# GpSimd in source order, and masks formed from one broadcast of the decay logs per pair

## The chip, the cores and the metric

The kernel runs on one core of a Trainium2 chip. The metric is the device time of one execution in microseconds (us); of several runs the median is given. A core has a matrix engine (TensorE, PE in the views), a vector engine (VectorE, DVE), a scalar engine (ScalarE, ACT) and GpSimd (POOL). Each works through a queue of its own in a fixed order, and so does SyncE (SP), which only issues DMAs here. An instruction that waits holds up everything behind it in its queue. The PE clock has two levels, 1.2 and 2.4 GHz; the views give the granted clock as a share of 2.4 GHz, so that 0.50 is the lower level.

## The reference

Attention with a multiplicative decay for 8 batches x 8 heads, 576 tokens, head width 64, followed by a token-mixing and feed-forward block. What matters here, for one head:

```python
scores = (q @ k.T) / sqrt(D)
cum = cumsum(log(clip(f, 1e-4, 1.0)))          # running sum of the decay logs
scores = where(causal, -1e9, scores + cum[:, None] - cum[None, :])
attn = exp(scores - rowmax(scores)); attn /= attn.sum(-1)
x = attn @ v                                   # heads side by side: 576 x 512 a batch
h = x.T @ U @ V;  u = x + h.T
out = u + relu(u @ w_ch1) @ w_ch2
```

Within a row `cum[i]` is a constant that the softmax removes, so the kernel adds only the key's term `cum[j]` (scaled by -8) and the causal mask.

## The kernel before

Two heads make a **pair**, 32 pairs in all, four to a batch. `step(t)` handles pair p = t in ten slots s = 0 to 9: scores of row blocks 3, 1, 0 in slot 0 (`run_a`), of row block 2 and of the 64 tail rows in slot 3 (`run_b`), and the transposes of the exponentials P in slots 4 to 9 (`turn_p`). In the same ten slots it finishes the pair before, a = t - 1: the inverse of the row sums (`inverse`, tiles `sm` and `rv`) in slot 1, values in slot 3 (`values`), transposes back (`turn_x`, `turn_last`, tiles Tx and Tz) in slots 5 and 6, a split in high and low parts (`split_x`, tiles xh and xl) in slot 7 and the rank products (`ranks`, tile Tt) in slot 9. Matmuls of the feed-forward part of the batch before fill the slots (tiles A and B), and the first step after a batch's last pair also holds that batch's mixing (tiles H and Tu); steps 9, 13, 17, 21, 25 and 29 are such.

On VectorE, `top` (L290, L335) adds the mask tile to the scores in PSUM and finds the row extreme; ScalarE then forms P (L299). Each transposed block goes through a bank of the two-bank pool `psT` (tiles T) and is copied to `PT`, by ScalarE (first group) or VectorE (L366, the second and third groups). The division `rv` (L359) multiplies the result when Tx and Tz are taken out of their banks (L437, L402).

A pair's masks: four main tiles `M{p}_{i}` of 128 rows x 2 heads x 128(i+1) keys and one tail tile `M{p}_t`. `load_masks(p + 2)` in slot 5 has SyncE broadcast the logs from HBM (`cumd`) into each of them; each has two buffers, so a tile's DMA for pair p + 2 waits for `top` of pair p, which read that buffer. `triangles(p + 1)` in slots 4 and 7 has GpSimd write the masked triangle into the diagonal 128 columns (L142, L146).

`manual_schedule(engines=...)` names the engines whose queue keeps the order of the source. PE has it throughout, SyncE in step 0 and from step 8. VectorE, ScalarE and GpSimd are ordered by a list scheduler with estimates of its own, within the waits that the data need. So their queues aren't in the order in which the code is written.

Of the kernel before, what the change touches and what calls it, by code (L numbers as in the profile page):

```python
# [8 lines left out]
F32 = mybir.dt.float32  # L9
# [5 lines left out]
ALU = mybir.AluOpType  # L15
PSUM = bass.MemoryType.PSUM
ET = mybir.EngineType

B, H, S, D = 8, 8, 576, 64
# [3 lines left out]
P = 128  # L23
NHP = H // 2
NM = 4
MAIN = NM * P
TAIL = S - MAIN
# [7 lines left out]
MASKED = -8.0e9  # L35
# [6 lines left out]
def tile_decay_attention_moe(ctx, tc, qk, v, f, U, V, w1, w2, out):  # L42
    nc = tc.nc

    cumd = nc.dram_tensor("cumd", (B * H, S), F32, kind="Internal").ap()
# [45 lines left out]
    sb = pool("sb")  # L91
    sb2 = pool("sb2", 2)
# [8 lines left out]
    OWN = (slice(0, 64), slice(64, 128))  # L101
# [11 lines left out]
    make_identity(nc, ident)  # L113
    xn = [cst.tile([P, NM + 1, DM], F32, name=f"xn{i}") for i in range(NX)]

    def load_masks(p):
        if p >= NP:
            return
        z = st.setdefault(p, {"M": {}})
        for i in (3, 1, 0, 2):  # L120
            w = P * (i + 1)
            m = z["M"][i] = sb2.tile([P, 2, w], F32, tag=f"M{i}", name=f"M{p}_{i}")
            if p == 0:
                nc.gpsimd.memset(m, 0.0)
            else:
                src = cumd.rearrange("(j p) s -> p j s", j=2)[p, :, 0:w]
                nc.sync.dma_start(m, src.unsqueeze(0).broadcast_to([P, 2, w]))
        m = z["M"][NM] = sb2.tile([P, S], F32, tag="Mt", name=f"M{p}_t")
        if p == 0:
            nc.gpsimd.memset(m, 0.0)  # L130
            return
        for j in range(2):
            nc.sync.dma_start(m[OWN[j]], cumd[j * B * NHP + p].unsqueeze(0).broadcast_to([64, S]))

    def triangles(p, rows):
        if p >= NP:
            return
        for i in rows:
            m = st[p]["M"][i]
            if i < NM:  # L140
                d = m[:, :, P * i : P * i + P]
                nc.gpsimd.affine_select(d, d, [[0, 2], [-1, P]], ALU.is_ge, MASKED, base=0, channel_multiplier=1)  # L142
                continue
            for j in range(2):
                d = m[OWN[j], MAIN:S]
                nc.gpsimd.affine_select(d, d, [[-1, TAIL]], ALU.is_ge, MASKED, base=0, channel_multiplier=1)  # L146

    w1h = wt.tile([P, NA, NDC, P], F32R, name="w1h")
    w1l = wt.tile([P, NA, NDC, P], F32R, name="w1l")
# [72 lines left out]
    st = {}  # L222
# [405 lines left out]
    with tc.manual_schedule(engines=None):  # L628
        stay_awake(12)
        fr = sb.tile([P, S], F32, tag="xT", name="fr")  # L630
        fl = sb.tile([P, S], F32, tag="xh", name="fl")
        fl0 = sb2.tile([P, 10], F32, tag="sm", name="fl0")[:, 0:1]
        for j in range(2):
            nc.sync.dma_start(fr[OWN[j]], f)
        nc.scalar.activation(fl0, warm[:, 0:1], AF.Ln)
        load_qk(0)
        load_w(0)
        nc.vector.tensor_scalar(fr, fr, 1e-4, 1.0, op0=ALU.max, op1=ALU.min)
        nc.scalar.activation(fl, fr, AF.Ln)
        nc.scalar.activation(fl0, warm[:, 0:1], AF.Exp)  # L640
        picks = sb.tile([P, 2 * P], F32, tag="qkl", name="picks")
        n = B * NHP
        for rows, cols, col in (
            (OWN[0], slice(0, P), 0), (OWN[1], slice(0, P), 64 + n),
            (slice(0, P), slice(P, P + 64), 0), (slice(0, P), slice(P + 64, 2 * P), 64 + n),
        ):
            own = ident[rows, col : col + 1]
            nc.vector.tensor_scalar(picks[rows, cols], warm[rows, cols], own, -8.0, op0=ALU.mult, op1=ALU.mult)
        load_masks(0)
        triangles(0, range(NM + 1))  # L650
        nc.vector.tensor_tensor_scan(fr, fl, fl, 0.0, op0=ALU.add, op1=ALU.bypass)
        load_qk(1)
        load_w(1)
        nc.vector.tensor_scalar(fl[0 : B * H], fr[0 : B * H], -8.0, None, op0=ALU.mult)
        nc.sync.dma_start(cumd, fl[0 : B * H])
        load_masks(1)
        load_v(0)
        for i in range(NX - 1):
            nc.gpsimd.memset(xn[i][64:128, NM, :], 0.0)
# [29 lines left out]
    def step(t):  # L689
        p = SEQ[t]  # L690
        a = SEQ[t - 1] if t else None
        ps_, pa = p is not None, a is not None
        last, ending = t == LAST, t > LAST - 2
        nxt_p = p + 1 if ps_ else NP
        if ps_:
            z = st[p]
# [3 lines left out]
        for s in range(8 if last else SLOTS):  # L700
# [23 lines left out]
                stay_awake(1)  # L724
            if s == 4 and ps_ and p:
                load_v(p)
            if s == 4 and ps_:
                triangles(p + 1, (3, 1, 0))
            if s == 6 and ps_:
                load_qk(p + 2)  # L730
                if p == 0:
                    load_w(2)
                    load_w(3)
            if s == 5 and ps_:
                load_masks(p + 2)
            if s == 7 and ps_:
                triangles(p + 1, (2, NM))

            if ps_ and s == 0:
                run_a(p)  # L740
# [39 lines left out]
    pending = []  # L780
    ROOM = (1, 2, 3, 4, 5, 6, 8, 9)
    credit = [0.0]
    with tc.manual_schedule(engines={ET.PE, ET.SP}):
        step(0)
    with tc.manual_schedule(engines={ET.PE}):
        for t in range(1, 8):
            step(t)
    with tc.manual_schedule(engines={ET.PE, ET.SP}):
        for t in range(8, LAST + 1):
            step(t)  # L790
        run_later()
# [247 lines left out]
    z = {"g": order[0], "acc": xn[1], "po": [None] * NM, "done": [0] * NM}  # L1039
# [248 lines left out]
    with tc.manual_schedule(engines={ET.PE, ET.DVE, ET.Activation}):  # L1288
# [4 lines left out]
        s = 0  # L1293
# [8 lines left out]
        while batch_of(s) or queue or drains or any(x >= s for x in later):  # L1302
# [30 lines left out]
            for h, k, j, how in batch:  # L1333
                m = pairs[k].m
# [13 lines left out]
            for h, k, j, how in batch:  # L1348
                p = pairs[k]
# [7 lines left out]
            for h, k, j, how in batch:  # L1357
                p = pairs[k]
# [28 lines left out]
            while queue and queue[0][0] <= s and (credit > (1.0 if pairs[queue[0][1]].plain else 0.5)):  # L1387
                at, k, x = queue.pop(0)
                p = pairs[k]
# [63 lines left out]
```

## Time and profile before

| | |
|---|---|
| runs | 1456.59, 1459.94, 1461.51 us; median 1459.94 |
| profiled execution | 1459.31 us, of which its span is 1457.5 us |
| PE busy | 1221.3 us, 84% of the span |
| PEld (weight loads, overlap PE) | 1046.2 us, 72% |
| DVE busy | 841.4 us, 58% |
| ACT busy | 632.5 us, 43% |
| POOL busy | 257.8 us, 18% |
| mean granted PE clock | 0.915 |
| DMA | 218.76 MB, mean 150 GB/s |

Busy shares are averages over stages with different limits: the pairs run from 7 us to some 930 us, and the rest is the feed-forward part in another form. What each engine waits for has to be read stage by stage.

### The profile page before, as it was taken

The numbers are of one execution on the slowest core, as the hardware profiler recorded it, in microseconds if no ns is written. First come the engines' busy times: TensorE is split into PE (matmuls) and PEld (weight loads), VectorE is DVE, ScalarE is ACT, GpSimd is POOL, SyncE is SP. The second block draws the span as 40 slices with busy tenths as digits, with TensorE's granted clock in tenths as the row PEclk, the third lists the DMA queues.
The fourth block names the chain that finished last, engine by engine and source line by source line (L and its number), as shares of the span: only waits on it lengthen the run. The fifth ranks groups of instructions, "written<-read, shape, count | busy, mean of one in ns | idle before, by whom it ended". The sixth has DMA issues, their size and how long they took to land.

```text
span 1457.5 us, 24048 instructions
## 1 busy us (share of the span) xinstructions
PE 1221.3 (84%) x8465; PEld 1046.2 (72%) x8465; DVE 841.4 (58%) x2151; ACT 632.5 (43%) x1675; POOL 257.8 (18%) x423
## 2 busy tenths in 40 slices
PE   6554788777769768976876879999999999999998
PEld 3332567656567557765765657898788999999998
DVE  4464744533445434543443357698677678767775
ACT  3343444433334333442443335343455555555563
POOL 3343523112322222223212321000000000000000
PEclk8676798889979988988898989999999999999999
DMA  7855644655565565453352454459667575566534
GB/s 170 191 128 126 162 92 106 136 114 91 119 143 108 89 173 91 103 143 110 85 169 85 113 111 150 169 169 309 214 203 238 172 239 178 175 205 212 173 116 122
DMA packets 150281, 218.76 MB, mean 150 GB/s; under 512 B 17488, under 2 KB 83536, under 8 KB 148112
## 3 DMA queue, kind: packets, MB, share of 16 engines
q1 hardware_dynamic: 149888, 216.96, 55.3%
q8 instruction: 67, 1.10, 0.3%
q14 instruction: 54, 0.44, 0.1%
q10 hardware_dynamic: 272, 0.26, 0.1%
HBM read 169.84 MB, written 47.33 MB: 149 GB/s over the span
## 4 chain that ended last, share of the span: by engine, by line
PE 54%; DMA 25%; DVE 9%; issue 4%; ACT 4%; POOL 3%; SPq 1%; POOLq 0%; DVEq 0%; ACTq 0%
DMA M_t<-cumd 16%; PE pf L1093 13%; PE po L1185 7%; PE A L572 5%; PE B L590 5%; DMA M<-cumd 4%; PE V L420 4%; PE px L1185 3%; PE T L379 3%; ACT P L299 2%; PE pf L1185 2%; PE Tt L470 2%; PE Hb L916 2%; PE S_0c L278 1%; PE po L1200 1%
## 5 line engine op out<-in xcount | busy, mean ns | idle before, releaser
L379 PE MATMUL T<-ident,P 128*128 128x128 f32 x640 | 119.7, 318 | 159.7 <-DVE PT L366 150.9
L379 PEld LDWEIGHTS T<-ident,P 128*128 128x128 f32 x640 | 89.7, 164 | 182.6 <-issue 159.2
L1316 ACT COPY mc<-pf 128x512 f32<-128x512 f32 x139 | 81.5, 586 | 169.0 <-PE pf L1093 169.0
L142 POOL TENSOR_SCALAR_AFFINE_SELECT M<-M 128x256 f32<-128x256 f32 x128 | 52.6, 412 | 534.8 <-DMA M<-cumd 500.6
L572 PE MATMUL A<-uh,w1h 128*128 128x256 f32 (+1 forms) x384 | 124.2, 323 | 1.8 <-DVE hl L576 1.8
L420 PE MATMUL V<-PT,vr 128*64 128x448 f32 (+3 forms) x640 | 99.7, 453 | 22.4 <-ACT PT L364 18.9
L572 PE MATMUL A<-ul,w1h 128*128 128x256 f32 (+1 forms) x384 | 117.4, 306 | 0.3 <-DVE ul L510 0.3
L572 PE MATMUL A<-uh,w1l 128*128 128x256 f32 (+1 forms) x384 | 117.3, 306 | 0.0
L359 DVE RECIPROCAL rv<-sm 128x9 f32<-128x9 f32 x32 | 6.9, 215 | 176.2 <-POOL sm L358 176.2
L366 DVE COPY PT<-T 128x256 f32<-128x256 f32 (+1 forms) x192 | 73.6, 414 | 49.9 <-PE T L379 49.1
L590 PE MATMUL B<-w2h,hh 128*128 128x512 f32 x216 | 94.9, 439 | 3.3 <-DVE ost L604 3.3
L420 PEld LDWEIGHTS V<-PT,vr 128*64 128x64 f32 x640 | 42.6, 144 | 75.9 <-issue 37.5
L1244 POOL TENSOR_TENSOR xn<-xn,xn 128x512 f32<-128x512 f32 x1 | 1.3, 1267 | 529.8 <-DMA out_dram<-xn 529.8
L453 ACT CAST xh<-xn 128x640 fp32r<-128x640 f32 x32 | 23.2, 726 | 161.7 <-DVE xn L402 161.7
L590 PE MATMUL B<-w2l,hh 128*128 128x512 f32 x216 | 88.1, 408 | 0.0
L590 PE MATMUL B<-w2h,hl 128*128 128x512 f32 x216 | 87.8, 407 | 0.0
L572 PEld LDWEIGHTS A<-uh,w1h 128*128 128x128 f32 x384 | 76.7, 200 | 2.4 <-DVE hl L576 2.0
L576 DVE SCALAR_TENSOR_TENSOR hl<-A,hh 128x256 fp32r<-128x256 f32 (+1 forms) x96 | 43.4, 452 | 58.3 <-ACT hh L580 58.2
L572 PEld LDWEIGHTS A<-uh,w1l 128*128 128x128 f32 x384 | 76.9, 200 | 0.1
L572 PEld LDWEIGHTS A<-ul,w1h 128*128 128x128 f32 x384 | 76.4, 199 | 0.5 <-DVE ul L510 0.5
L160 POOL TENSOR_TENSOR qkl<-raw,qkh 128x1216 fp32r<-128x1216 f32 x26 | 72.1, 2772 | 20.5 <-ACT qkh L157 20.5
L1093 PE MATMUL pf<-d,b1h 128*128 128x256 f32 x320 | 69.6, 280 | 1.3 <-DVE fd L921 1.3
(322 smaller groups left out, 3904.2 us busy)
## 6 DMA issues: line engine op xcount, KB each, us to landing
un<-ud SPq DMA_DIRECT2D x16, 1024.0 KB, 7.0
M<-cumd SPq DMA_DIRECT2D x31, 512.0 KB, 5.8
d<-ud SPq DMA_DIRECT2D x48, 256.0 KB, 3.9
M<-cumd SPq DMA_DIRECT2D x31, 384.0 KB, 8.6
twd<-xn SPq DMA_DIRECT2D x40, 256.0 KB, 2.8
raw<-in_qk_dram SPq DMA_DIRECT2D x32, 288.0 KB, 7.8
Th<-twd SPq DMA_DIRECT2D x35, 256.0 KB, 3.6
tw<-twd SPq DMA_DIRECT2D x35, 256.0 KB, 2.8
```

Of the source, the lines that this page charges most:

```text
L142: nc.gpsimd.affine_select(d, d, [[0, 2], [-1, P]], ALU.is_ge, MASKED, base=0, channel_multiplier=1)
L160: leng.tensor_tensor(dl, src, dh.bitcast(F32), op=ALU.subtract)
L299: nc.scalar.activation(pt, ps, AF.Exp, bias=z["nm"][:, col : col + 1], scale=-1.0, accum_out=z["sm"][:, col : col + 1])
L366: defer(2, lambda: nc.vector.tensor_copy(dst, src))
L379: nc.tensor.transpose(tp[:, P * (x + c) : P * (x + c) + P], z["P"][j][i][:, P * c : P * c + P], ident)
L420: nc.tensor.matmul(ps, vr[:, c, j], pt[:, j, c, lo:hi], start=c == 0, stop=lo == 0)
L572: nc.tensor.matmul(ps[:, :nt], wt[:, fc, c], ut[:, c, sl], start=m == 0, stop=m == 3 * NDC - 1)
L576: nc.vector.scalar_tensor_tensor(hl[:, fc, :nt], ps[:, :nt], 0.0, hh.bitcast(F32)[:, fc, :nt], op0=ALU.max, op1=ALU.subtract)
L590: nc.tensor.matmul(ps, ht[:, fc, P * x : P * x + P], wt[:, fc], start=fc == 0 and m == 0, stop=fc == NA - 1 and m == 2,)
L1093: nc.tensor.matmul(ps, a[x][:, c], b[y][:, c], start=start and m == 0, stop=m == 5, skip_group_check=True)
L1185: nc.tensor.matmul(ps[:, HT * x : HT * x + HT], f[a][:, P * x : P * x + P], w[b], start=k.i == 0 and m == 0 and x == 0 and not (k.n == NG ...
L1316: nc.scalar.copy(mc, FA)
```

## The change

Two things. First, GpSimd is added to the engines that keep the source's order, in all steps. Second, SyncE broadcasts one tile a pair, `decay` (2 heads x 512 keys, two buffers), and GpSimd forms each of the four main masks from it with one `affine_select` that writes the whole tile, logs and triangle. The main mask tiles now have one buffer instead of two. The tail tile is broadcast as before. The masks of pair p + 1 are formed in slots 2, 3, 4, 6 and 8 of step p.

```diff
-    def load_masks(p):
+    def load_decay(p):
         if p >= NP:
             return
         z = st.setdefault(p, {"M": {}})
-        for i in (3, 1, 0, 2):
-            w = P * (i + 1)
-            m = z["M"][i] = sb2.tile([P, 2, w], F32, tag=f"M{i}", name=f"M{p}_{i}")
-            if p == 0:
-                nc.gpsimd.memset(m, 0.0)
-            else:
-                src = cumd.rearrange("(j p) s -> p j s", j=2)[p, :, 0:w]
-                nc.sync.dma_start(m, src.unsqueeze(0).broadcast_to([P, 2, w]))
+        z["decay"] = sb2.tile([P, 2, MAIN], F32, tag="decay", name=f"decay{p}")
         m = z["M"][NM] = sb2.tile([P, S], F32, tag="Mt", name=f"M{p}_t")
         if p == 0:
+            nc.gpsimd.memset(z["decay"], 0.0)
             nc.gpsimd.memset(m, 0.0)
             return
+        src = cumd.rearrange("(j p) s -> p j s", j=2)[p, :, 0:MAIN]
+        nc.sync.dma_start(z["decay"], src.unsqueeze(0).broadcast_to([P, 2, MAIN]))
         for j in range(2):
             nc.sync.dma_start(m[OWN[j]], cumd[j * B * NHP + p].unsqueeze(0).broadcast_to([64, S]))
 
-    def triangles(p, rows):
+    def mask(p, i):
         if p >= NP:
             return
-        for i in rows:
-            m = st[p]["M"][i]
-            if i < NM:
-                d = m[:, :, P * i : P * i + P]
-                nc.gpsimd.affine_select(d, d, [[0, 2], [-1, P]], ALU.is_ge, MASKED, base=0, channel_multiplier=1)
-                continue
-            for j in range(2):
-                d = m[OWN[j], MAIN:S]
-                nc.gpsimd.affine_select(d, d, [[-1, TAIL]], ALU.is_ge, MASKED, base=0, channel_multiplier=1)
+        z = st[p]
+        if i < NM:
+            w = P * (i + 1)
+            m = z["M"][i] = sb.tile([P, 2, w], F32, tag=f"M{i}", name=f"M{p}_{i}")
+            nc.gpsimd.affine_select(
+                m, z["decay"][:, :, 0:w], [[0, 2], [-1, w]], ALU.is_ge, MASKED, base=P * i, channel_multiplier=1
+            )
+            return
+        for j in range(2):
+            d = z["M"][NM][OWN[j], MAIN:S]
+            nc.gpsimd.affine_select(d, d, [[-1, TAIL]], ALU.is_ge, MASKED, base=0, channel_multiplier=1)
...
-            if s == 4 and ps_:
-                triangles(p + 1, (3, 1, 0))
+            if s in MASKS and ps_:
+                mask(p + 1, MASKS[s])
...
             if s == 5 and ps_:
-                load_masks(p + 2)
-            if s == 7 and ps_:
-                triangles(p + 1, (2, NM))
+                load_decay(p + 2)
...
-    with tc.manual_schedule(engines={ET.PE, ET.SP}):
+    MASKS = {2: 3, 3: 1, 4: 0, 6: 2, 8: NM}
+    with tc.manual_schedule(engines={ET.PE, ET.SP, ET.Pool}):
         step(0)
-    with tc.manual_schedule(engines={ET.PE}):
+    with tc.manual_schedule(engines={ET.PE, ET.Pool}):
         for t in range(1, 8):
             step(t)
-    with tc.manual_schedule(engines={ET.PE, ET.SP}):
+    with tc.manual_schedule(engines={ET.PE, ET.SP, ET.Pool}):
         for t in range(8, LAST + 1):
             step(t)
```

The queue of PE is the same row for row before and after. What moves on the others is shown at three places. The numbers that stand first in a name are the pair's (M9_3 is the mask of pair 9, row block 3; sm7 and rv7 the sums and inverse of pair 7); the last number is a buffer's.

GpSimd before, from the masks of pair 9 on:

```order
L142 AFFINE_SELECT M9_3_1875<-M9_3_1875 128x2x128
L142 AFFINE_SELECT M9_1_1877<-M9_1_1877 128x2x128
L142 AFFINE_SELECT M9_0_1879<-M9_0_1879 128x256
L160 TENSOR_TENSOR qkl8_1872<-raw0_88,qkh8_1871 128x1216
L142 AFFINE_SELECT M9_2_1881<-M9_2_1881 128x2x128
L146 AFFINE_SELECT M9_t_1883<-M9_t_1883 64x64
L357 TENSOR_TENSOR sm7_1728<-sm7_1728 128x1
L146 AFFINE_SELECT M9_t_1883<-M9_t_1883 64x64
L358 TENSOR_SCALAR sm7_1728<-sm7_1728 128x9
L360 COPY rv7_2040<-rv7_2040 64x1
L454 TENSOR_TENSOR xl6_1936<-xn1_106,xh6_1935 128x512
L456 TENSOR_TENSOR xh6_1935<-xn1_106,xh6_1935 64x128
```

The same stretch of GpSimd in the change:

```order
L138 AFFINE_SELECT M9_3_2041<-decay9_1856 128x1024
L138 AFFINE_SELECT M9_1_2063<-decay9_1856 128x512
L138 AFFINE_SELECT M9_0_2114<-decay9_1856 128x256
L158 TENSOR_TENSOR qkl9_2140<-raw1_89,qkh9_2139 128x1216
L138 AFFINE_SELECT M9_2_2175<-decay9_1856 128x768
L452 TENSOR_TENSOR xl7_2201<-xn1_106,xh7_2200 128x512
L454 TENSOR_TENSOR xh7_2200<-xn1_106,xh7_2200 64x128
L144 AFFINE_SELECT M9_t_1857<-M9_t_1857 64x64 x2
L355 TENSOR_TENSOR sm8_1969<-sm8_1969 128x1
L356 TENSOR_SCALAR sm8_1969<-sm8_1969 128x9
L358 COPY rv8_2299<-rv8_2299 64x1
```

Before, the sums of pair 7 stood behind all masks of pair 9, whose tiles are loaded into the buffers of pair 7. Now the masks of pair 9 stand with the work of step 8, ahead of the sums of pair 8, and the low part `xl7` stands ahead of the tail mask and the sums.

VectorE before, around the inverse of pair 8 (T8_01 to T8_12 are banks with transposed blocks of pair 8, Tz7 the last transpose of pair 7):

```order
L366 COPY PT8_2139<-T8_01_2206 128x2x128
L366 COPY PT8_2139<-T8_01_2206 128x128
L576 SCALAR_TENSOR_TENSOR hl0_256_1917<-A0_256_5_2185,hh0_256_1916 128x256
L402 TENSOR_TENSOR xn1_106<-Tz7_2210,rv7_2040 64x128
L359 RECIPROCAL rv8_2325<-sm8_1993 128x9
L366 COPY PT8_2139<-T8_11_2237 128x2x128
L366 COPY PT8_2139<-T8_11_2237 128x128
L366 COPY PT8_2139<-T8_02_2243 128x3x128
L366 COPY PT8_2139<-T8_12_2248 128x3x128
```

VectorE in the change at that place:

```order
L364 COPY PT8_2118<-T8_01_2183 128x2x128
L364 COPY PT8_2118<-T8_01_2183 128x128
L574 SCALAR_TENSOR_TENSOR hl0_256_1896<-A0_256_5_2158,hh0_256_1895 128x256
L400 TENSOR_TENSOR xn1_106<-Tz7_2187,rv7_2016 64x128
L364 COPY PT8_2118<-T8_11_2205 128x2x128
L364 COPY PT8_2118<-T8_11_2205 128x128
L364 COPY PT8_2118<-T8_02_2217 128x3x128
L364 COPY PT8_2118<-T8_12_2222 128x3x128
L475 TENSOR_TENSOR TS1_1421<-Tt7_2226,TS1_1421 32x128
L357 RECIPROCAL rv8_2299<-sm8_1969 128x9
L288 ISA S9_0c_2248,nm9_2242<-S9_0c_2248,M9_3_2041 128x512
```

The inverse moved from the middle of the step, ahead of copies that free transpose banks, to its end, just ahead of the next pair's first `top`. It moves so for 30 of the 32 pairs; a few neighbours that change places apart, nothing else moves on VectorE.

SyncE before, the loads around the masks of pair 11:

```order
L263 DMA vr1_95<-in_v_dram 128x4x128
L264 DMA vr1_95<-in_v_dram 64x128
L127 DMA M11_3_2431<-cumd 128x2x512
L127 DMA M11_1_2433<-cumd 128x2x256
L127 DMA M11_0_2435<-cumd 128x2x128
L127 DMA M11_2_2437<-cumd 128x2x384
L133 DMA M11_t_2439<-cumd 64x576 x2
L248 DMA raw1_89<-in_qk_dram 128x576
```

SyncE in the change:

```order
L261 DMA vr1_95<-in_v_dram 128x4x128
L262 DMA vr1_95<-in_v_dram 64x128
L127 DMA decay11_2408<-cumd 128x2x512
L129 DMA M11_t_2409<-cumd 64x576 x2
L246 DMA raw1_89<-in_qk_dram 128x576
```

One broadcast of 512 KB takes the place of four of 1280 KB together; the places of the other loads stay.

## Rows read from the trace of the kernel before

**Rows 1.** The page: PE clock granted, in tenths, in 40 slices of the span.
```profile
PEclk8676798889979988988898989999999999999999
```

**Rows 2.** Windows: length, PE, PEld, DVE, ACT, POOL busy, PEclk, DMA share, GB/s.
```profile
15.83:182.21 166.38, 93.85 (x485) 59.03 (x484) 90.38 (x234) 62.15 (x175) 67.74 (x100) 0.70 0.66 150
182.21:901.46 719.25, 569.23 (x3888) 466.34 (x3886) 325.57 (x986) 277.29 (x813) 177.80 (x294) 0.90 0.51 116
901.46:1457.50 556.04, 543.95 (x4038) 513.85 (x4037) 415.12 (x904) 285.10 (x666) 4.28 (x7) 1.00 0.59 192
```

**Rows 3.** The same view of three single steps: 18, 20 and 21.
```profile
520.27:554.82 34.55, 24.65 (x181) 21.04 (x179) 12.54 (x41) 11.64 (x37) 7.13 (x12) 0.85 0.61 157
581.49:606.54 25.05, 23.75 (x162) 19.29 (x161) 13.02 (x40) 11.03 (x33) 7.21 (x12) 1.00 0.54 99
606.54:639.10 32.56, 21.96 (x144) 17.44 (x145) 15.50 (x42) 11.41 (x31) 7.12 (x12) 0.84 0.31 95
```

**Rows 4.** Waits in steps 6 to 30: who waited for whom, us, times, longest.
```profile
POOL M L142 <- DMA M<-cumd: 420.6, 88, 18.0
...
DVE rv L359 <- POOL sm L358: 151.2, 24, 12.5
...
PE T L379 <- DVE PT L366: 125.7, 24, 10.7
```

**Rows 5.** The chain that ended last, in step 18: start us, us, what.
```profile
531.32 0.53 DVE S_1t L335
...
531.96 13.77 DMA M_t<-cumd
...
546.64 0.26 POOL sm L358
...
547.14 0.49 DVE PT L366 x2
...
547.76 1.30 PE T L379 x5
```

**Rows 6.** PE in order of time: first and last of 16 waits above 3 us.
```profile
203.88 0.97 PE L379 MATMUL T<-ident,P 128*128 128x128 f32 x6 [3.49 <-DVE PT L366]
...
869.32 0.88 PE L379 MATMUL T<-ident,P 128*128 128x128 f32 x3 [7.62 <-DVE PT L366]
```

**Rows 7.** Busy time just after the waits in steps 18 and 21, columns as in rows 2.
```profile
547.70:553.30 5.60, 5.54 (x25) 4.89 (x25) 2.50 (x7) 1.01 (x2) 1.73 (x2) 0.50 0.01 3
632.70:639.10 6.40, 4.94 (x31) 4.90 (x33) 4.91 (x12) 2.06 (x4) 1.90 (x3) 0.53 0.14 52
```

**Rows 8.** Waits in steps 1 to 5.
```profile
PE T L379 <- DVE PT L366: 25.2, 10, 10.2
...
PE V L420 <- ACT PT L364: 18.9, 4, 8.4
...
PE Tx L435 <- ACT PT L364: 10.1, 4, 4.6
```

**Rows 9.** GpSimd's groups by shape: count, busy us, mean ns of one, idle before.
```profile
L142 POOL TENSOR_SCALAR_AFFINE_SELECT M<-M 128x256 f32<-128x256 f32 x128 | 52.6, 412 | 534.8 <-DMA M<-cumd 500.6 <-DVE nm L335 18.8 <-DVE nm L290 4.6
...
masks.py:199 POOL TENSOR_SCALAR_AFFINE_SELECT ident<-ident 128x128 f32<-128x128 f32 x1 | 0.3, 302 | 0.0
```

**Rows 10.** Instructions and loads of tiles M: ns min/median/max, landing in us.
```profile
L142 POOL TENSOR_SCALAR_AFFINE_SELECT M<-M x128: 402/406/637, 4.6 to 866.2; 128x256 f32<-128x256 f32 x128
...
L290 DVE CUSTOM_DVE_ANT_0 S_1c<-S_1c,M x32: 675/695/734, 9.7 to 903.1; 128x512 f32<-128x512 f32 x32
...
DMA to landing us min/median/max: 5.1/8.2/13.8
```

**Rows 11.** A decode step of the weights on VectorE, ns min/median/max.
```profile
L71 DVE SCALAR_TENSOR_TENSOR xn<-xn x10: 671/692/3114, 114.8 to 914.0; 128x512 f32<-128x512 uint32 x10
```

**Rows 12.** The low part of queries and keys on GpSimd, ns min/median/max.
```profile
L160 POOL TENSOR_TENSOR qkl<-raw,qkh x26: 2742/2762/2819, 150.4 to 887.9; 128x1216 fp32r<-128x1216 f32 x26
```

**Rows 13.** GpSimd's split of the results, by shape.
```profile
L454 POOL TENSOR_TENSOR xl<-xn,xh 128x512 fp32r<-128x512 f32 x31 | 40.3, 1300 | 43.3 <-ACT xh L453 38.3 <-DVE xn L74 4.5
```

More of the change, by code (lines that the diff above doesn't have):

```diff
@@ L648, in tile_decay_attention_moe @@
             nc.vector.tensor_scalar(picks[rows, cols], warm[rows, cols], own, -8.0, op0=ALU.mult, op1=ALU.mult)
-        load_masks(0)
-        triangles(0, range(NM + 1))
+        load_decay(0)
+        for i in (3, 1, 0, 2, NM):
+            mask(0, i)
         nc.vector.tensor_tensor_scan(fr, fl, fl, 0.0, op0=ALU.add, op1=ALU.bypass)
@@ L655, in tile_decay_attention_moe @@
         nc.sync.dma_start(cumd, fl[0 : B * H])
-        load_masks(1)
+        load_decay(1)
         load_v(0)
```

## The prediction

> **What bounds the kernel now.** I read the windows first, cut at the first score matmul of steps 1, 6 and 31. The last stretch, 556 us, is TensorE's: 544 us busy at full clock [rows 2], and the change touches nothing there. In steps 6 to 30 TensorE is busy 569 of 719 us at a mean clock of 0.90, in steps 1 to 5 only 94 of 166 us at 0.70. So 222 us are idle, and part of the busy time runs at the lower level, 1.2 GHz; the slices of the page show where [rows 1]. No other engine is full in steps 6 to 30: VectorE has 326 us, GpSimd 178.
>
> Single steps come next. Step 20 needs 25.05 us with TensorE busy 23.75 at clock 1.00, while 18 and 21 need 34.55 and 32.56 us at 0.85 and 0.84 with no more work in them [rows 3]. The list of waits names what they lose: TensorE waits 125.7 us in 24 pieces for VectorE's copies L366 to free a transpose bank, and VectorE waits 151.2 us in as many pieces for GpSimd's row sums [rows 4]. GpSimd itself waits for the masks' DMAs. The chain through step 18 shows that these are one wait: the tail `top` of pair 18 (531.32), then the DMA of pair 20's tail mask into the buffer just freed (13.77 us), GpSimd's triangle, its sums of pair 18, which stand behind that triangle, the inverse, two copies, and at 547.76 the transposes go on [rows 5]. That is a queue's order and no need of the data: those sums have no use for a mask of pair 20, and the copies have no use for the inverse.
>
> **What the change moves, part by part.** First, the order. GpSimd now takes the masks of pair p + 1 in step p, from loads issued in slot 5 of step p - 1, and the sums of pair p in slot 1 of step p + 1. VectorE's inverse moves from ahead of the second and third groups of copies to the end of the step, behind the rank part `TS`. To get there VectorE has waited for Tt, which needs `xl` and `xh` from GpSimd; after these GpSimd has two tail triangles and two sums left, about 1 us. So the inverse finds its sums ready or nearly so, and nothing that frees a bank stands behind it. I cost the inverse's wait at nothing and the 125.7 us as removed.
>
> Second, the clock. After the stall in step 18 TensorE runs 5.60 us at 0.50, 5.54 of them busy [rows 7], and then at the full level. Work done at half clock takes twice as long, so this stretch loses 2.8 us. 16 of the 24 waits are above 3 us (first and last in [rows 6]) and I give each such a tail: 16 x 2.8 = 45 us. Step 20, with a short wait only, stayed at 1.00 [rows 3].
>
> Third, what is late next. When the stall goes, the rest of the step must run at full clock behind VectorE. In step 21, one of the six steps with mixing, VectorE had 4.91 us of work between 632.70 and 639.10, TensorE 4.94 us at a mean clock of 0.53 [rows 7], which is 2.6 at the full level. The difference, 2.3 us, can come out as waits for banks; I put 2 us for each of the six. The other 19 steps hold fewer copies and more matmuls, and I put 0.5 us. That gives back 6 x 2 + 19 x 0.5 = 21 us.
>
> Fourth, the masks themselves. `affine_select` takes 302 ns for 128 columns and 412 ns for 256 [rows 9], 0.86 ns a column; by that line the whole tiles of 1024, 512, 256 and 768 columns take 1.07, 0.63, 0.41 and 0.85 us, 2.97 us a pair against 4 x 0.41 = 1.65. A tile that wide isn't in the trace; from below a mask could cost what a diagonal costs, from above twice my line, 5.9 us. GpSimd is busy 178 of 719 us [rows 2], so 33 us or 106 us more in 25 steps hide beside TensorE. Where that cover is gone is slot 7: the masks, `qkl` (2.76 us [rows 12]) and the split stand in one queue, and `xl` needs 1.30 us [rows 13] before the rank matmuls of slot 9. Up to `xl` a step asks 2.97 + 2.76 = 5.7 us of GpSimd, in seven slots of over 2 us each, so it is there in time. The one-buffer masks make GpSimd wait for VectorE's `top` of the same step (slot 2 for a `top` of slot 1); that delays masks needed a step later, and `qkl`, needed in the next slot 0. Nothing at either bound, unless the queue runs late as a whole.
>
> Fifth, the loads. Four broadcasts of 1280 KB a pair become one of 512 KB. SyncE no longer waits for `top` before it issues them, since `decay` of pair p was used up a step earlier. A mask load lands in 5.1 to 13.8 us [rows 10]; it has from slot 5 to slot 2 of the next step, 7 slots or some 15 us. DMA share is 0.51 [rows 2], so what fewer bytes give is at most small, and I count nothing. In the first step one mask of 1.07 us takes the place of a triangle of 0.41 on the path, 0.7 us, left out.
>
> Sixth, steps 1 to 5. The same waits for copies sum to 25.2 us, and waits of V and Tx for ScalarE to 18.9 and 10.1 [rows 8]. ScalarE there holds weight decodes whose middle part is GpSimd's, queued behind triangles as well. They also depend on their own loads and on VectorE, busy 90 of 166 us. I take two thirds of the 54.2 us as removed, 36, and of the clock half: 93.85 us of work at 0.70 would be 66 at full clock, 28 us less, so 14. Bounds: 15 us (some of the copies' waits alone) and 54 + 28 = 82.
>
> **The sum.** 125.7 + 45 - 21 + 36 + 14 = 199 us. The profiled execution took 1459.3 us (1.8 of it outside its span), which is the median of the runs within 0.6 us: 1459.3 - 199 = **1260 us**.
>
> **A rule against it.** VectorE's L71 reads tiles in SBUF only; its longest instance took 3114 ns where the median is 692 [rows 11]. The masked reduction L290, which takes one input from PSUM, stayed within 675 and 734 ns over 32 instances [rows 10], in steps full of GpSimd work. The Trainium skill, page "SBUF — State Buffer", section "Who interferes with whom", says why the first can be: GpSimd shares a port pair with VectorE as an exclusive lock, and an instruction with two SBUF inputs is shut out while GpSimd reads SBUF. By that rule the longer masks can hurt only the weight decodes, and the sum stays; the trace agrees.
>
> **The rivals.**
> VectorE takes over: every step's second half is as VectorE-bound as I read in step 21, 2.3 us x 25 = 58 instead of 21, and gaps of that size bring the low clock back, so that the 45 us don't come. 1260 + 37 + 45 = 1342 us. For it: VectorE 4.91 of 6.40 us in rows 7. Against: step 20, with 13.0 us of VectorE, kept the full clock.
> The masks shut VectorE out, whatever it reads: 25 + 6 pairs x 1.3 us more is 41 us, all masks 31 x 2.97 = 92. From 1301 to 1352. Against: L290's narrow times.
> The new order frees nothing: the sums now stand behind the tail mask of the next pair, and if that load lands as late as its forerunner did, VectorE waits as before; some 1455 us. Against: that load is issued a whole step earlier.
> Slower: `decay` late. One load now gates all four masks, and behind them `qkl` and `xl` stand in the same queue, so a late load stops the next scores and the rank matmuls. Issue to use is some 15 us, GpSimd's room ahead of `xl` about 5; the gain is 199 / 25 = 8 us a step. So it decides from about 28 us after the issue. At 33 us every step loses 5 more: 1459 + 25 x 5 = 1584. Against: 13.8 us is the longest landing seen [rows 10].
>
> **How the numbers follow.** Forecast 0.74, with a range of its own from 1225 (steps 1 to 5 at their upper bound) to 1310; VectorE takes over 0.12; shut out 0.07; nothing freed 0.03; slower 0.04. Below, with nothing given back and steps 1 to 5 at 82, it would be 1459.3 - 125.7 - 45 - 82 = 1206. So the range is 1205 to 1345: it takes in the second rival and most of the third, and leaves out somewhat over 1 in 10. Faster by over 0.3% (about what a measurement of this kernel tells from no change) has the first three cases and half of the fourth, 0.94; same 0.02; slower 0.04.
>
> **What the profile of the change would show.** The wait of `rv` for `sm` near nothing, and that of T for L366 below some 25 us in steps 6 to 30; steps such as 18 and 21 at 22 to 24 us and step 20 still near 25; the granted clock at 1.00 in most of them; a mask of 1024 columns at about 1.07 us; the last stretch still 556 us. I would be wrong if T waited for copies that themselves wait for nothing but VectorE's queue, if Tt waited for `xl` by more than 1 us a step, or if GpSimd stood waiting for `decay`.

## The result and the profile after

The changed kernel takes 1270.28 us (median of 4 runs, 1269.93 to 1272.35), the kernel before on the same chip 1458.26 us; the ratio is 0.8712, with an interval of 0.8691 to 0.8732. That is 10 us above the forecast of 1260 and inside the range. The profiled execution took 1269.93 us, 1268.0 of it span. One execution among the runs below, the profiled one of broadcast_only, ran at a mean granted clock of 0.56 and took 1883 us, so the time given for that kernel is the median of its other three and its rows come from a second run of it, broadcast_again.

The page of the changed kernel, its clock slices [rows 1] and its line on the loads of `decay`, with KB of one and us to landing:

```profile
PEclk8876899999999999999999999999999999999999
...
decay<-cumd SPq DMA_DIRECT2D x31, 512.0 KB, 5.3
```

The windows of steps 1 to 5, 6 to 30 and the rest, columns as in [rows 2]:

```profile
16.07:155.36 139.29, 91.04 (x486) 57.17 (x485) 90.54 (x233) 63.04 (x175) 73.42 (x93) 0.74 0.47 135
155.36:714.41 559.05, 528.92 (x3888) 429.44 (x3887) 326.49 (x985) 277.23 (x813) 212.39 (x301) 1.00 0.40 117
714.41:1268.00 553.59, 543.54 (x4038) 513.73 (x4037) 415.36 (x905) 285.08 (x666) 4.44 (x9) 1.00 0.59 193
```

Against [rows 2] the three stretches gave 27.1, 160.2 and 2.4 us. Steps 6 to 30 divide into two gains: TensorE's idle time went from 719.25 - 569.23 = 150.0 to 559.05 - 528.92 = 30.1 us, and its busy time from 569.2 to 528.9, for the same count of matmuls, at a granted clock of 1.00 in place of 0.90.

Steps 18, 20 and 21 [rows 3]:

```profile
418.66:441.11 22.45, 21.86 (x181) 18.83 (x178) 12.54 (x42) 11.65 (x37) 9.11 (x16) 1.00 0.68 207
463.62:487.45 23.83, 23.65 (x162) 19.39 (x161) 13.17 (x40) 11.02 (x33) 8.41 (x12) 1.00 0.15 50
487.45:509.68 22.23, 20.22 (x144) 15.38 (x145) 15.10 (x41) 11.39 (x31) 7.71 (x9) 1.00 0.34 101
```

TensorE is busy for nearly all of each now, and 18 and 21 are ten to twelve us shorter. The waits of steps 6 to 30 [rows 4] say why:

```profile
POOL M L138 <- DVE nm L288: 65.0, 24, 5.7
...
PE T L377 <- DVE PT L364: 9.3, 15, 1.7
...
DVE rv L357 <- POOL sm L356: 4.3, 7, 0.9
```

Of the inverse's wait of 151.2 us 4.3 are left, of the transposes' 125.7 us 9.3. GpSimd, which stood 420.6 us waiting for mask DMAs, waits for none here; it waits for VectorE's `top` before it may write the one-buffer masks, as the prediction said, and no wait of TensorE for GpSimd stands in the list of these steps.

### The profile page after: what moved, and what is told of

It reads as the page before. It is cut to its first block, busy times and chain, and to the rows that moved or that the text cites. A ratio compares the mean times of both kernels' runs of the same rounds, so it can differ in the third digit from the quotient of the medians.

```text
span 1268.0 us, 23680 instructions
## 1 busy us (share of the span) xinstructions
PE 1178.0 (93%) x8465; PEld 1007.4 (79%) x8465; DVE 841.9 (66%) x2151; ACT 633.3 (50%) x1675; POOL 297.2 (23%) x420
## 4 chain that ended last, share of the span: by engine, by line
PE 68%; ACT 10%; DVE 8%; issue 6%; POOL 4%; DMA 3%; SPq 0%; POOLq 0%; ACTq 0%; DVEq 0%
PE pf L1091 16%; PE B L588 8%; PE po L1183 8%; PE A L570 8%; PE V L418 7%; ACT P L297 5%; PE px L1183 4%; PE T L377 3%; PE po L1198 2%; PE pf L1183 2%; PE Hb L914 2%; DMA decay<-cumd 2%; PE O L930 2%; PE S_0b L276 1%; ACT PT L362 1%
## 5 line engine op out<-in xcount | busy, mean ns | idle before, releaser
L377 PE MATMUL T<-ident,P 128*128 128x128 f32 x640 | 102.5, 284 | 23.6 <-DVE PT L364 16.9
L570 PE MATMUL A<-uh,w1h 128*128 128x256 f32 (+1 forms) x384 | 120.1, 313 | 1.7 <-DVE hl L574 1.7
L570 PE MATMUL A<-uh,w1l 128*128 128x256 f32 (+1 forms) x384 | 113.8, 296 | 0.0
L138 POOL TENSOR_SCALAR_AFFINE_SELECT M<-decay 128x1024 f32<-128x1024 f32 (+3 forms) x128 | 93.4, 751 | 78.1 <-DVE nm L288 65.6
L377 PEld LDWEIGHTS T<-ident,P 128*128 128x128 f32 x640 | 77.6, 145 | 42.6 <-issue 10.4
L588 PE MATMUL B<-w2h,hh 128*128 128x512 f32 x216 | 90.7, 420 | 3.3 <-DVE ost L602 3.3
L570 PEld LDWEIGHTS A<-uh,w1h 128*128 128x128 f32 x384 | 73.4, 191 | 2.4 <-DVE hl L574 2.0
L570 PEld LDWEIGHTS A<-uh,w1l 128*128 128x128 f32 x384 | 73.6, 192 | 0.1
L297 ACT ACTIVATE P<-S_0b,nm 128x384 f32<-128x384 f32 x32 | 18.6, 582 | 109.3 <-DVE nm L288 109.3
L578 ACT ACTIVATE hh<-A 128x256 fp32r<-128x256 f32 (+1 forms) x96 | 40.2, 419 | 56.1 <-PE A L570 56.1
```

What stands on the lines that cost most here:

```text
L138: nc.gpsimd.affine_select(m, z["decay"][:, :, 0:w], [[0, 2], [-1, w]], ALU.is_ge, MASKED, base=P * i, channel_multiplier=1)
L297: nc.scalar.activation(pt, ps, AF.Exp, bias=z["nm"][:, col : col + 1], scale=-1.0, accum_out=z["sm"][:, col : col + 1])
L377: nc.tensor.transpose(tp[:, P * (x + c) : P * (x + c) + P], z["P"][j][i][:, P * c : P * c + P], ident)
L570: nc.tensor.matmul(ps[:, :nt], wt[:, fc, c], ut[:, c, sl], start=m == 0, stop=m == 3 * NDC - 1)
L588: nc.tensor.matmul(ps, ht[:, fc, P * x : P * x + P], wt[:, fc], start=fc == 0 and m == 0, stop=fc == NA - 1 and m == 2,)
```

## The experiments

My theory when I set them up: the time lost was the row sums, standing in GpSimd's queue behind the tail mask of a later pair, and GpSimd's source order takes them out of there; the fewer bytes of the loads count for nothing. The rival: the queue's order is indifferent, and what counts is how late the tail mask lands, because of what is loaded ahead of it. A third reading, that longer masks hold VectorE, was still to be ruled out. All times are medians in us; each chip has its own time of the kernel before.

| run | time | ratio to before, 95% interval |
|---|---|---|
| first chip, before 1458.21 | | |
| order_only | 1291.88 | 0.8858 [0.8818, 0.8898] |
| broadcast_only | 1281.82 | 0.8783 [0.8742, 0.8824] |
| masks_twice | 1285.25 | 0.8803 [0.8762, 0.8843] |
| order_from_6 | 1270.12 | 0.8706 [0.8669, 0.8743] |
| second chip, before 1470.04 | | |
| broadcast_again | 1286.27 | one execution |
| bo_spare_loads | 1448.49 | 0.9869 [0.9822, 0.9915] |
| spare_loads | 1298.84 | 0.8840 [0.8812, 0.8869] |
| decode_137 | 1267.95 | 0.8623 [0.8591, 0.8655] |
| third chip, before 1470.45 | | |
| sums_on_vector | 1400.30 | 0.9532 [0.9504, 0.9560] |
| tail3 | 1470.11 | 1.0003 [0.9979, 1.0026] |
| after_again (the changed kernel) | 1270.45 | 0.8648 [0.8626, 0.8670] |
| decode_137_again | 1267.96 | 0.8627 [0.8604, 0.8650] |

### The two halves of the change, each alone

**order_only** is the kernel before with GpSimd in source order, and no other edit:

```diff
-    with tc.manual_schedule(engines={ET.PE, ET.SP}):
+    with tc.manual_schedule(engines={ET.PE, ET.SP, ET.Pool}):
         step(0)
-    with tc.manual_schedule(engines={ET.PE}):
+    with tc.manual_schedule(engines={ET.PE, ET.Pool}):
         for t in range(1, 8):
             step(t)
-    with tc.manual_schedule(engines={ET.PE, ET.SP}):
+    with tc.manual_schedule(engines={ET.PE, ET.SP, ET.Pool}):
         for t in range(8, LAST + 1):
```

> The kernel before with one edit: GpSimd keeps the source's order in all steps. Four broadcasts a pair, two buffers a mask and diagonal triangles stay. Queue theory (the gain is that the row sums no longer stand behind a mask of a later pair): 1270 to 1285 us, steps 6 to 30 at 560 to 570 us, wait of the inverse for the sums under 10 us in these steps. Load theory (the gain comes from one broadcast instead of four, fewer bytes and a SyncE that waits for no buffer): at most half of the gain, 1365 us or more.

It took 1291.88 us, 166 less than before, a little over the queue theory's 1270 to 1285. The tail masks land as late as before (median 8.8 us, longest 16.8, against 8.4 and 15.1), and TensorE doesn't feel it. GpSimd in one step of order_only:

```profile
404.85 1.28 POOL L454 TENSOR_TENSOR xl<-xn,xh 128x512 fp32r<-128x512 f32 x1 [2.46 <-ACT xh L453]
...
407.10 0.54 POOL L146 TENSOR_SCALAR_AFFINE_SELECT M_t<-M_t 64x64 f32<-64x64 f32 x2
407.72 0.20 POOL L357 TENSOR_TENSOR sm<-sm 128x1 f32<-128x1 f32 x1
408.00 0.25 POOL L358 TENSOR_SCALAR sm<-sm 128x9 f32<-128x9 f32 x1
```

The tail mask written here was issued a step earlier, so it is there (no bracket: no wait). But the sums still stand behind a tail mask, and they still come late in the step. In step 20 GpSimd ends them 22.7 us after the step's first score matmul in order_only and 22.3 us after it in the changed kernel (485.90), later than the 19.5 us in the kernel before (600.95). What has changed for TensorE is VectorE's queue, whose inverse the scheduler now puts behind the copies. VectorE in the same step of order_only, then in step 20 of the kernel before and of the changed one:

```profile
405.39 0.62 DVE L366 COPY PT<-T 128x256 f32<-128x256 f32 x2 [1.37 <-PE T L379]
...
407.42 0.56 DVE L366 COPY PT<-T 128x384 f32<-128x384 f32 x1 [0.62 <-PE T L379]
408.29 0.21 DVE L359 RECIPROCAL rv<-sm 128x9 f32<-128x9 f32 x1 [0.31 <-POOL sm L358]
```

```profile
600.99 0.22 DVE L359 RECIPROCAL rv<-sm 128x9 f32<-128x9 f32 x1 [2.93 <-POOL sm L358]
601.12 0.56 DVE L366 COPY PT<-T 128x256 f32<-128x256 f32 x2
```

```profile
481.21 0.62 DVE L364 COPY PT<-T 128x256 f32<-128x256 f32 x2 [1.01 <-PE T L377]
...
485.94 0.22 DVE L357 RECIPROCAL rv<-sm 128x9 f32<-128x9 f32 x1
```

So source order doesn't free the copies by bringing the sums early: with the inverse behind them, the copies wait for no sums. Together with `xl`, which now stands ahead of the tail mask, that is what the order gives. No run moves the inverse alone, so the share of each is read from the rows and not shown by a run.

**broadcast_only** is the change without GpSimd's source order (the three `ET.Pool` are left out).

> The changed kernel with one edit: GpSimd is ordered by the scheduler again; one broadcast a pair, whole masks and one buffer stay. Queue theory: the sums of a pair stand behind the tail mask of the pair after next or next but one, whose load waits for the tail reduction, so most of the wait stays: 1380 to 1440 us, steps 6 to 30 at 650 to 710 us. Load theory: 1270 to 1300 us.

1281.82 us: 98 us below the lower end of what my theory allowed, and inside the load theory's range. The scheduler still puts the sums behind a tail mask and the inverse ahead of the copies, and yet nearly the whole gain is there.

> The kernel of the run before this one that had the broadcast alone, once more for a profile at the usual clock. Its time, 1283 us, went against the queue theory as I put it. Landing theory: the sums still stand behind a tail mask of a later pair, but that load lands some 5 us after the tail reduction, since 768 KB less stand ahead of it, so the inverse waits for the sums by 1 to 2 us a step instead of 6. Order theory: with masks that wait for the reduction of the step, the scheduler's GpSimd order itself became harmless, and the inverse doesn't wait at all, however late the tail mask lands.

GpSimd in one step of broadcast_again:

```profile
438.87 2.79 POOL L158 TENSOR_TENSOR qkl<-raw,qkh 128x1216 fp32r<-128x1216 f32 x1 [0.53 <-DMA decay<-cumd]
441.81 0.23 POOL L144 TENSOR_SCALAR_AFFINE_SELECT M_t<-M_t 64x64 f32<-64x64 f32 x1 [0.15 <-DVE hl L574]
442.02 0.19 POOL L355 TENSOR_TENSOR sm<-sm 128x1 f32<-128x1 f32 x1
442.72 0.24 POOL L144 TENSOR_SCALAR_AFFINE_SELECT M_t<-M_t 64x64 f32<-64x64 f32 x1 [0.51 <-DMA M_t<-cumd]
443.05 0.25 POOL L356 TENSOR_SCALAR sm<-sm 128x9 f32<-128x9 f32 x1
```

The second row of sums (L356) stands behind the tail's triangles as it did before, but their wait for the DMA is half a us. The tail mask lands in 3.2 us (median; before 8.4), and the inverse's wait for the sums is 30.5 us in 30 pieces, some 1 us each, as the landing theory has it. So the chain can be cut at a second place, the landing, and the half that I had counted at nothing cuts it there.

### Putting the bytes back

To see whether the landing hangs on the bytes ahead of it, three loads of 256, 128 and 384 KB (the size that the change saves) go between `decay` and the tail mask, into tiles that nobody reads:

```diff
         nc.sync.dma_start(z["decay"], src.unsqueeze(0).broadcast_to([P, 2, MAIN]))
+        for i in (1, 0, 2):
+            spare = sb.tile([P, 2, P * (i + 1)], F32, tag=f"spare{i}", name=f"spare{p}_{i}")
+            nc.sync.dma_start(spare, src[:, 0 : P * (i + 1)].unsqueeze(0).broadcast_to([P, 2, P * (i + 1)]))
```

**bo_spare_loads** does so in broadcast_only.

> The broadcast alone (GpSimd ordered by the scheduler), and beside it three loads of 256, 128 and 384 KB a pair from the same logs into tiles that nobody reads, between decay and the tail mask, so that bytes and number of loads are those of before. Landing theory: the tail mask lands 4 us later and the inverse waits for the sums again: 1340 to 1420 us. Order theory: 1283 us within 10.

1448.49 us: of the 184 us that broadcast_again is below the kernel before on this chip, 162 are lost again, more than expected. In steps 6 to 30 of bo_spare_loads the waits, and GpSimd in one of the steps (its line numbers are higher by three):

```profile
DVE rv L360 <- POOL sm L359: 140.2, 24, 12.7
POOL M_t L147 <- DMA M_t<-cumd: 137.8, 36, 12.1
PE T L380 <- DVE PT L367: 69.7, 15, 10.9
...
PE Tu L520 <- DVE ul L511: 43.9, 6, 8.6
```

```profile
521.85 2.79 POOL L161 TENSOR_TENSOR qkl<-raw,qkh 128x1216 fp32r<-128x1216 f32 x1 [0.53 <-ACT qkh L158]
536.71 0.23 POOL L147 TENSOR_SCALAR_AFFINE_SELECT M_t<-M_t 64x64 f32<-64x64 f32 x1 [12.07 <-DMA M_t<-cumd]
536.92 0.19 POOL L358 TENSOR_TENSOR sm<-sm 128x1 f32<-128x1 f32 x1
```

TensorE's wait for the copies is smaller than before (69.7 for 125.7 us) because in the six steps with mixing it stops at Tu instead, for VectorE's `ul`, which stands behind the inverse there. From step 6 on GpSimd's instructions stand in the same order in the two kernels, the same sums behind the same triangles; the three loads make the triangle wait 12.07 us instead of half a us, and the landing 8.5 us (longest 15.3) instead of 3.2. They bring back the 768 KB and three more transfers at once, so which of the two counts is not shown.

**spare_loads** puts the same loads into the changed kernel, where GpSimd keeps source order.

> The changed kernel with the same three loads a pair into tiles that nobody reads. If source order makes the step independent of when masks land, steps 6 to 30 stay at 559 us within 5 and the time at 1270 to 1285 us. If the 768 KB a pair cost time by themselves (other loads land later), 1300 us or more.

1298.84 us, some 28 more than the changed kernel and between the two outcomes. Its windows of steps 1 to 5 and 6 to 30:

```profile
16.09:175.53 159.44, 89.73 (x486) 55.84 (x485) 90.63 (x233) 63.47 (x175) 73.52 (x93) 0.73 0.69 161
175.53:742.21 566.68, 531.03 (x3889) 430.86 (x3887) 326.70 (x985) 277.73 (x813) 212.82 (x301) 0.99 0.68 146
```

The tail mask lands late again (median 9.4 us, longest 16.7), and steps 10 to 29 take what they took in the changed kernel, to 0.1 us. 9 us come in step 30 (35.9 for 27.1), 20 in steps 1 to 5. In source order, then, the middle of the kernel doesn't feel when masks land; step 30 and the first steps do.

**tail3** asks whether it is the wait for its own freed buffer that makes the tail mask late, the link from `top` to the DMA in the chain that I read [rows 5]. It is the kernel before with a third buffer for the tail mask:

```diff
-        m = z["M"][NM] = sb2.tile([P, S], F32, tag="Mt", name=f"M{p}_t")
+        m = z["M"][NM] = sb3.tile([P, S], F32, tag="Mt", name=f"M{p}_t")
```

> The kernel before, with a third buffer for the tail mask, so that its load no longer waits for VectorE's top of the pair that used the buffer. If the wait for the freed buffer is what makes the tail mask late (the first link of the chain that the prediction read), the time falls below 1380 us. If the tail mask is late because of the 1280 KB issued just ahead of it on SyncE's queue, its issue moves by under 1 us and the time stays at 1440 to 1465 us, with T's wait for copies still near 125 us.

1470.11 us, a ratio of 1.0003. The whole profile's wait of T for copies is 154.1 us in 33 pieces (before, both stretches together, 125.7 + 25.2), and the landing is 9.9 us. So the tail's `top` was the release that the chain showed, but not what the time hung on. SyncE's waits in the kernel before say why:

```profile
SPq L127 <- DVE nm L290: 224.6, 58, 12.1
...
SPq L133 <- DVE nm L335: 19.5, 24, 1.0
```

The tail's load never waited more than 1.0 us for its buffer, since the four main loads just ahead of it on the queue wait for theirs. Those waits stay in tail3 (227.2 us), and no run takes them alone away; but in bo_spare_loads the broadcast and the spare loads ahead of the tail wait for buffers some 7 us in all of steps 6 to 30, and the mask lands as late.

### A third cut, and what it left

**sums_on_vector** leaves loads and masks as before and lets VectorE do the two additions that the inverse waits for; otherwise both queues stay, but for the inverse and its last column's copy L360, which change places with a few neighbours:

```diff
-        nc.gpsimd.tensor_tensor(sm[:, 8:9], sm[:, 8:9], sm[:, 9:10], op=ALU.add)
-        nc.gpsimd.tensor_scalar(sm[:, 0:9], sm[:, 0:9], 1e-9, None, op0=ALU.add)
+        nc.vector.tensor_tensor(sm[:, 8:9], sm[:, 8:9], sm[:, 9:10], op=ALU.add)
+        nc.vector.tensor_scalar(sm[:, 0:9], sm[:, 0:9], 1e-9, None, op0=ALU.add)
```

> The kernel before, with only the two additions of the row sums moved from GpSimd to VectorE, where they stand directly ahead of the inverse; loads, masks and both queues' order stay. If the gain is the chain of the sums behind a later pair's tail mask (my theory), a third way to cut it must give most of it too: VectorE's inverse waits for nothing from GpSimd, T's wait for copies in steps 6 to 30 falls from 125.7 us to under 30, and the time comes out at 1285 to 1310 us. If GpSimd's late masks hold up the step by a second way as well (the copy of the inverse's last column, or xl, both still behind the tail triangles), it stays above 1340 us.

1400.30 us: the second of the two outcomes, only 70 us gained. Steps 6 to 30 of sums_on_vector, their window and two of their waits:

```profile
185.00:840.40 655.40, 556.95 (x3886) 451.58 (x3885) 341.68 (x1035) 278.99 (x813) 167.07 (x244) 0.94 0.58 127
```

```profile
PE Tt L470 <- POOL xl L454: 70.2, 21, 6.5
...
PE T L379 <- DVE PT L366: 9.6, 16, 1.7
```

T's wait for copies is gone as far as in the changed kernel (9.6 us here, 9.3 there), as my theory says. But a wait that was 5.4 us in the whole of the kernel before, none of it in these steps, takes its place: the rank matmuls Tt wait for `xl`. GpSimd in one step shows where `xl` is:

```profile
514.45 0.23 POOL L146 TENSOR_SCALAR_AFFINE_SELECT M_t<-M_t 64x64 f32<-64x64 f32 x1 [0.38 <-DMA M_t<-cumd]
514.89 0.24 POOL L146 TENSOR_SCALAR_AFFINE_SELECT M_t<-M_t 64x64 f32<-64x64 f32 x1 [0.20 <-DMA M_t<-cumd]
515.18 0.18 POOL L360 COPY rv<-rv 64x1 f32<-64x1 f32 x1
515.45 1.26 POOL L454 TENSOR_TENSOR xl<-xn,xh 128x512 fp32r<-128x512 f32 x1
```

It stands behind the same triangles as the sums did. Before, T was stopped first, which held up everything after it, so nobody was seen waiting for `xl`. The change and order_only mend both: the inverse stands behind the copies, and `xl` ahead of the tail mask.

### The masks, and the first five steps

**masks_twice** writes each of the four main masks twice, the whole suspected cost doubled:

```diff
+            for _ in range(2):
+                nc.gpsimd.affine_select(
+                    m, z["decay"][:, :, 0:w], [[0, 2], [-1, w]], ALU.is_ge, MASKED, base=P * i, channel_multiplier=1
+                )
```

> The changed kernel with every main mask written twice, the same values over themselves, so GpSimd has 3.0 us more a pair (93 us in all). Cover theory (GpSimd's time hides beside TensorE from step 6 on, and only delays the early steps, where weight decodes share its queue): steps 6 to 30 longer by at most 5 us, steps 1 to 5 by 5 to 15, 1275 to 1290 us. Shut-out theory (masks hold VectorE off): about 90 us more, 1360 us, and VectorE's masked reductions of 128x512 well above 0.7 us.

Steps 6 to 30 of masks_twice:

```profile
166.66:726.47 559.81, 530.20 (x3887) 430.92 (x3887) 326.16 (x983) 277.24 (x813) 286.19 (x404) 0.99 0.40 116
```

74 us more of GpSimd work cost 0.8 us here (559.81 for 559.05), and VectorE's busy time didn't move; the reduction of 512 columns with one input in PSUM took 676 to 700 ns. Of the 15.2 us by which the profiled span is longer, 10.7 come in steps 1 to 5 (150.03 us for 139.29) and 3.1 after step 30. That masks shut VectorE out of its reductions falls. In the changed kernel L71, both of whose inputs are in SBUF, still has an instance of 3058 ns, which begins while GpSimd forms a `qkl` of 2.76 us; four others, in steps 2 to 4, begin beside masks and took 1.20 to 1.48 us instead of some 0.69. Of the two kinds, L71 is the one for which the Trainium skill, page "SBUF — State Buffer", section "Who interferes with whom", expects a lock, and the trace agrees.

**order_from_6** keeps the scheduler's order for GpSimd in steps 0 to 5, to see what source order does there.

> The changed kernel, but GpSimd keeps the source's order from step 6 on only; in steps 0 to 5 the scheduler orders it. If source order is what gained 27 us in steps 1 to 5, these go back towards 166 us and the time to 1285 to 1297 us. If the low part xl behind the weight decodes costs more there than the sums behind masks did, they shrink to some 125 us and the time to 1255 us. Steps 6 to 30 at 559 us either way.

Neither outcome came: steps 1 to 4 take 112.69 us, 112.67 in the changed kernel, and the time is the same. The loads alone give what is gained there: broadcast_again takes 138.76 us in steps 1 to 5, order_only 151.93, the changed kernel 139.29.

**decode_137** follows a wait that has grown in the changed kernel, from 5.4 to 14.6 us. TensorE's waits in its steps 1 to 5 [rows 8]:

```profile
PE Tt L468 <- POOL xl L452: 14.6, 3, 5.5
PE V L418 <- ACT PT L362: 10.8, 4, 4.1
PE T L377 <- DVE PT L364: 7.6, 10, 1.4
...
PE Tx L433 <- ACT PT L362: 2.9, 4, 1.4
```

GpSimd at the end of step 2, and TensorE's row that waits for it, in the changed kernel:

```profile
60.65 2.71 POOL L138 TENSOR_SCALAR_AFFINE_SELECT M<-decay 128x1024 f32<-128x1024 f32 x3
63.33 1.42 POOL L72 TENSOR_TENSOR stg<-stg 128x576 f32<-128x576 f32 x1
65.53 1.49 POOL L74 TENSOR_TENSOR VV<-stg,VV 32x576 fp32r<-32x576 f32 x1 [0.78 <-ACT VV L73]
67.09 0.90 POOL L138 TENSOR_SCALAR_AFFINE_SELECT M<-decay 128x768 f32<-128x768 f32 x1
67.96 1.69 POOL L452 TENSOR_TENSOR xl<-xn,xh 128x512 fp32r<-128x512 f32 x1
```

```profile
69.71 0.37 PE L468 MATMUL Tt<-xl,Us 128*64 128x128 f32 x1 [5.53 <-POOL xl L452]
```

ScalarE had finished `xh` at 61.05 (60.32 + 0.73 in its row), and `xl` started at 67.96: three masks, two parts of a weight decode (L72, L74) and a fourth mask stand ahead of it. decode_137 moves the decodes of steps 2 to 4:

```diff
-    DECODES = [(0, 9), (1, 2), (1, 7), (2, 1), (2, 5), (2, 8), (3, 1), (3, 5), (3, 8), (4, 2), (4, 5), (4, 8), (5, 3)]
+    DECODES = [(0, 9), (1, 2), (1, 7), (2, 1), (2, 3), (2, 7), (3, 1), (3, 3), (3, 7), (4, 1), (4, 3), (4, 7), (5, 3)]
```

> The changed kernel with the weight decodes of steps 2 to 4 started in slots 1, 3 and 7 instead of 1 or 2, 5 and 8, so that GpSimd's part of a decode no longer stands between the masks and the low part xl. If xl behind a decode is what keeps TensorE idle at the ends of steps 2 to 4 (5.5, 3.9 and 5.1 us), these waits fall under 1 us each and steps 1 to 5 shrink by 12 to 20 us, 1250 to 1260 us. If the decodes bound these steps anyway, the same time is lost in other waits, 1270 us within 5.

Steps 1 to 5 shrink by 6.4 us (132.88), less than expected, and the wait for `xl` isn't the reason: it is still 14.5 us in 2 pieces. Then both kernels ran on one chip.

> The changed kernel once more, for comparison on this chip: a ratio to the kernel before of 0.869 to 0.874, 1266 to 1274 us.

> The changed kernel with the weight decodes of steps 2 to 4 in slots 1, 3 and 7, against the changed kernel on the same chip. If the 6 us that steps 1 to 5 lost in the first run of it are real, it is 3 to 8 us below the changed kernel with intervals that do not overlap; if they were one execution's scatter, the two agree within 3 us.

The changed kernel's time is as expected; its ratio is lower, since the kernel before takes longer here. The medians differ by 2.5 us, less than the 3 us set beforehand, the intervals overlap, and some 4 us of what steps 1 to 5 gain is given back after step 30. So it is not shown that decode_137 beats the change.

## Why the prediction was right, and where it was not

**The wait in steps 6 to 30.** I counted the 125.7 us of T's waits as removed; 116.4 went (9.3 are left). The signs came: the inverse's wait is 4.3 us, steps 18 and 21 take 22.45 and 22.23, the last stretch 553.6; only step 20, put near 25, is shorter too (23.83). What I wrote of the order is borne out: the inverse finds its sums nearly ready at the end of the step, and nothing that frees a bank stands behind it. It is this place of the inverse that frees T, and not earlier sums, as my theory of the experiments had it. order_only shows that GpSimd's order, with what the scheduler then does on VectorE, is enough. But the step "what fewer bytes give is at most small, and I count nothing" failed: broadcast_only shows that the one broadcast mends it too, and bo_spare_loads that the loss comes back with the loads it saves. The sum didn't show the error because the halves aren't additive: 166 us and 176 us alone, 188 together. On top of the broadcast, source order is worth about 12 us (steps 6 to 30 take 572.0 us in broadcast_again); on top of source order, the broadcast about 22 (12.6 of them in steps 1 to 5, 151.93 us in order_only).

**What was behind the sums.** I followed T alone. sums_on_vector shows that freeing T alone gives 70 us and turns 70 more into Tt's wait for `xl`. I had named Tt waiting for `xl` as a sign of being wrong, and the order rows show `xl` moved ahead of the tail mask, but I gave that move no price; the 125.7 us needed it.

**The clock.** 16 tails of 2.8 us made 45; TensorE's busy time fell by 40.3 us, so the sum made from one tail [rows 7] was a tenth too high.

**Given back.** I took off 21 us for VectorE behind the freed steps. TensorE's idle time with all of T's waits gone would be 150.0 - 125.7 = 24.3 us; it is 30.1, so some 5.8 came. VectorE's rate wasn't the error. The last 6.40 us of step 21 in the changed kernel, columns as in [rows 7]:

```profile
503.28:509.68 6.40, 5.87 (x49) 4.96 (x49) 5.88 (x13) 3.22 (x6) 2.99 (x6) 1.00 0.46 145
```

VectorE is busier here than just after the stall (5.88 us for 4.91), and yet TensorE is busy for 5.87 us at full clock, where I had given it 2.6 us of work beside VectorE's 4.91. What failed is the step from VectorE's excess to waits for banks: TensorE had other work to do in that time (49 matmuls here, 31 in [rows 7]), which in the kernel before was done ahead of the stall.

**Steps 1 to 5.** Here the sum was mis-sized: 50 forecast, 27.1 measured. Of the 54.2 us of waits in [rows 8], 32.9 went (7.6, 10.8 and 2.9 are left), but Tt's wait for `xl` grew from 5.4 to 14.6, so the idle time fell by 24.3 where I had put 36; and of the clock's 14 came 2.8: gaps of 4 to 5.5 us stayed in steps 2, 3 and 4, and the mean granted clock went from 0.70 to 0.74 only.

**The masks.** Forecast 1.07, 0.63, 0.41 and 0.85 us, measured 1.06, 0.65, 0.43 and 0.87. The widest, in GpSimd's groups by shape of the changed kernel (columns as in [rows 9]):

```profile
L138 POOL TENSOR_SCALAR_AFFINE_SELECT M<-decay 128x1024 f32<-128x1024 f32 x32 | 33.8, 1057 | 76.9 <-DVE nm L288 65.6 <-DMA decay<-cumd 11.3
```

The line through two narrow shapes held to four times the width. The one wait for `decay`, 11.3 us, is not in steps 6 to 30; so the slower rival, a late `decay` in every step, had no place, and at 5.3 us (median landing) it was far from its 28. That VectorE takes over (1342 us) did not come, and that the order frees nothing (1455) is excluded by order_only.

So steps 6 to 30 came out 10.5 us better than forecast, steps 1 to 5 by 23 us worse, the rest 2.4 better: 10 us in all. That the time came so close is in part luck, since the errors of 10.5 and 23 us had opposite signs. The lower end of the forecast's own range, 1225, is 1228 by its terms.

## What to carry to other kernels

An in-order engine whose queue holds an instruction that waits for a DMA passes that wait to everything behind it, and on to other queues whose next instruction needs one of those. Here it was cured by making the transfer land sooner, and also by an order in which neither VectorE's copies nor `xl` stood behind it; test each alone before you credit one, since together they don't add. Naming one engine in source order can reorder another that the scheduler still places, so compare the queues of all engines before you say what an edit did. When the first victim is freed, look in the same queue for the next: a wait that is small in the profile may be small only because another comes first. And a dense stretch of one engine costs time only if another has nothing else to do in it.

## What was not expected of the hardware

How soon a transfer lands went with what was issued ahead of it, though the DMA engines were far from full: the tail mask (two pieces of 144 KB) landed in a median of 3.2 to 3.3 us behind one load of 512 KB, at a DMA share of 0.38 to 0.40 in steps 6 to 30, and in 8.4 to 9.9 us behind 1280 KB, at 0.51 to 0.68, in six kernels, whatever GpSimd's order. Issuing it took longer too: SyncE's two instructions for it took 1.10 us together in a step of broadcast_again (from 438.61) and 4.90 in one of bo_spare_loads (from 521.59). And the kernel before took 1458 us with the result and on the first chip of the experiments and 1470 on the other two, while the changed one took 1270.28 with the result and 1270.45 on the third chip: the kernel with the stalls is the one that varied.
